# TensorE reads x with a step, from rows that land in zeroed buffers, in a kernel of attention and a state-space convolution mixed by a gate

## The chip, the cores and the metric

The kernel runs on one core of a Trainium2 chip, in one launch. The metric is the device time of that core in microseconds. A profiled execution gives, beside its time, the span from the first to the last instruction and a record of every instruction. The engines are named TensorE (PE in the profile, with its weight loads as PEld), VectorE (DVE), ScalarE (ACT), GpSimd (POOL) and SyncE (SP).

## The reference

The sequence has 2048 rows of 512 channels. Branch a is attention with 32 heads of 16, without a mask. Branch b is a diagonal state-space convolution of the same x along the sequence: for each channel a kernel K of length 2048 is made from 128 complex modes, and y is the causal convolution of K and x. A sigmoid gate of x mixes both.

```python
def _A_ref(x, wqkv, wo):                        # H = 32, Dh = 16
    q, k, v = split(x @ wqkv)
    p = softmax(einsum("bhqd,bhkd->bhqk", q, k) * Dh ** -0.5)
    return (p @ v).reshape(B, S, D) @ wo

def _B_ref(u, A_re, A_im, B_re, B_im, C_re, C_im, log_dt, Dskip):
    dt = exp(log_dt)[:, None]
    P = exp((dt * A)[:, :, None] * arange(L))
    K = einsum("dn,dnl,dn->dl", C, P, dt * Bc).real
    y = causal_convolution(K, u)                # by FFT in the reference
    return y + u * Dskip

x = A_x
g = sigmoid((x * gate_w).sum(-1, keepdims=True))
return g * _A_ref(x, ...) + (1 - g) * _B_ref(x, ...)
```

## The kernel before

**Attention.** The scores of one head for 512 queries and 128 keys are a slot; there are 2048 slots. A quad is four slots (four heads, one tile of keys). ScalarE takes the slots in groups of three: one instruction exponentiates 1536 columns from one of two PSUM buffers, SC0 and SC1, into the ring ET (`ex`, L705). TensorE makes the scores of the next group meanwhile (`qk`, "SC<-Qm,KT"), then PV (`pv`, "OA<-ET,VE"). Some quads are given to VectorE: then a group has two slots for ScalarE (1024 columns) and one that VectorE exponentiates by a polynomial in five instructions (`exp_in` L715, `exp_out` L725 to L732, result ED). Every 16 quads a block of queries is done: VectorE transposes OA (`norm_a`, L749), and TensorE's next PV waits for that. Qm (L681) is the masked Q of the next block.

**Convolution, in chunks of 64 rows.** Channels are taken in 16 blocks of 32, four blocks to a quarter. `params` and `base` make powers of the modes on VectorE; `base` ends a quarter with a cast (L944). `table` multiplies them out into PT (L968 copies, then six triples of two products tt and one PT, L763) and stores PT to DRAM (gm_ptd). `kstage` makes the taps of a block on TensorE ("MB<-PT,wrb" and "MB<-PT,nwi", eight matmuls) and stores a padded form (gm_kpd). `qload` reads PT back transposed (Qt). `sstage` makes, per block and in four banks, what each chunk adds to the state: 128 matmuls of 64 columns with x as the moving operand ("MB<-XZ,Qt"), and VectorE moves each bank to SG (L1051). `scan` runs over the 31 chunks in order on VectorE, five instructions a step (L1074 to L1087, the last a cast to SG). `ystage` makes y in 32 units: eight matmuls of 32 columns with x and the taps ("MB<-X,Tt"), then 32 with the states ("MB<-SG,Py", the moving operand read with a step of 288 elements).

**x for the convolution.** At the start x is copied to DRAM reordered (gm_xrd). For each quarter `ublocks` transfers two halves of 64 partitions into XS by SyncE's queue. VectorE gathers them so that the 32 chunks of a channel lie together (XP, L1178, two instructions), and writes two masked copies, one for each half of the partitions, into XZ (L1189, with the masks hm), so that one product of 64 columns keeps the two channels apart. `ulocal` transfers the same rows again into XR, and VectorE gathers them into X2 (L1178) for `ystage`.

**The order of the work.** The program for every engine is written out ahead by a planner (`Sched`). Each stage is a generator that yields the engine and an estimated cost of its next piece. After every exponential group the planner issues pieces whose inputs it thinks ready (`fill`), and pads TensorE with products of zeros ("OA<-wm") up to an amount of columns for each group. `dve_slot` gives VectorE a quad only when the taps of all blocks are done ("K15") and no quarter stands between its last state product and the end of its scan. The engines run their lists in order, with semaphores. SBUF is placed after planning (`place`): buffers whose lives don't meet share bytes, and the first use of one then waits for the last use of the other.

In `record`, what the change touches: the masks hm (L640, L641), the list of buffers (L991), the moving operands in `sstage` (L1047) and `ystage` (L1143), `rows` (L1170), `ublocks` (L1181) and `ulocal` (L1193).

```python
lambda k=k: XZ[qr](64 * (16 * bl + k), [[1, 64]]),
...
lambda kk=kk: X2[qr](32 * (16 * bl + kk), [[1, 32]]),
```

Of the kernel before, what the change touches and what calls it, by code (L numbers as in the profile page):

```python
# [6 lines left out]
FP32 = mybir.dt.float32  # L7
# [6 lines left out]
S = 2048  # L14
# [366 lines left out]
def declare(nc, es):  # L381
    B = {}

    def sb(name, free, dt=BF16):
        B[name] = Buf(name, "sb", free, dt)


    sb("KT", 4 * S)
    for k in range(16):
        sb(f"Q{k}", 512)  # L390
        sb(f"OnT{k}", 512)
    sb("Qm", 2 * 512)
    sb("VE", 64 * VW)
    sb("ET", NS * 512)
    sb("OT", 512, FP32)
    sb("ON", 512)
    sb("Rz", 2 * 16, FP32)
    sb("Wo", 4 * D)
    sb("xT", 4 * S)
    for n in ("Wk", "Wq", "Wv"):  # L400
        sb(n, 4 * D)
    sb("msk", 2, FP32)
    sb("sgn", 2, FP32)
    sb("hm", 2, FP32)
    sb("piota", 4, FP32)
    sb("hpi", 1, FP32)
    for k in range(EW):
        sb(f"eL{k}", 512, FP32)
    sb("em", 512, FP32)
    sb("eu", 512, FP32)  # L410
    sb("ED", 4 * 512)

    sb("gwT", 4)
    sb("wm", D)
    sb("x0n", 4 * D)
    sb("idf", P, FP32)
    sb("idb", P)
    sb("gp", NCH, FP32)
    sb("ge", NCH, FP32)
    sb("g", NCH, FP32)  # L420
    sb("g1", NCH, FP32)
    sb("Dpb", 16)
    sb("Dp", 16, FP32)
    sb("Yl", 16 * D)
    sb("fo", 4 * D)
    sb("fp", 4 * D, FP32)

    for n in ("AreT", "AimT", "BreT", "BimT", "CreT", "CimT", "ldt", "dt"):
        sb(n, D)
    for n in ("an", "bn", "ba", "ea", "e2", "sb_", "cb", "u1", "u2", "u3", "u4", "zr", "zi"):  # L430
        sb(n, D, FP32)
    sb("wrb", D)
    sb("nwi", D)
    sb("VV", 2 * D, FP32)
    sb("VL", 2 * D, FP32)
    for n in ("L1", "L2", "L4", "L8", "L16", "L32", "L48"):
        sb(n, 2 * D, FP32)
    sb("MU", 3 * D, FP32)
    sb("pt1", 2 * D, FP32)
    sb("pt2", 2 * D, FP32)  # L440
    for n in ("D16", "D32", "D48"):
        sb(n, 2 * 2 * D)

    sb("FP", 2 * 128 * 8, FP32)
    sb("ft1", 2 * 64 * 8, FP32)
    sb("ft2", 2 * 64 * 8, FP32)
    for k in range(4):
        sb(f"B16{k}", 2 * 128 * 16)

    sb("PT", 2 * 2 * CB * T)  # L450
    sb("tt1", 2 * CB * 16)
    sb("tt2", 2 * CB * 16)
    sb("Qt", 2 * 32 * 128)
    sb("Kst", 2 * 8 * P)

    for k in range(NSG):
        sb(f"SG{k}", NCH * 2 * SGH)
    sb("G", 2 * 128, FP32)
    for n in ("s2", "s3"):
        sb(n, 2 * 128, FP32)  # L460

    for k in range(4):
        sb(f"X2{k}", 32 * 64)
        sb(f"XZ{k}", 2 * 32 * 64)
        sb(f"XS{k}", 32 * 64)
        sb(f"XP{k}", 32 * 64)
        sb(f"XR{k}", 32 * 64)

    sb("Py", 3 * 2 * 16 * T)
    sb("Tt", 3 * 8 * 128)  # L470
    for i in range(2):
        B[f"SC{i}"] = Buf(f"SC{i}", "ps", 1536, FP32)
    B["OA"] = Buf("OA", "ps", 512, FP32)
    B["MB"] = Buf("MB", "ps", 512, FP32)
    for n, free in (("ptd", NBLK * P * 2 * CB * T), ("kpd", NBLK * P * 8 * P), ("xrd", S * D)):
        B[n] = Buf(n, "dr", free, BF16)
        B[n].t = nc.dram_tensor("gm_" + n, [free // P, P], BF16)
    for n in ("SC0", "SC1", "OA", "MB"):
        B[n].t = es.enter_context(nc.psum_tensor(n, [P, B[n].free], FP32))
    for n in ("x", "w", "wo", "are", "aim", "bre", "bim", "cre", "cim", "ldt_d", "dsk_d", "gw_d", "out"):  # L480
        B["d_" + n] = Buf("d_" + n, "dr", 1, BF16)
    return B
# [79 lines left out]
def record(nc, p, B, ins):  # L562
# [73 lines left out]
    for k in range(1, 8):  # L636
        op("DVE", lambda v, k=k: v.scalar_tensor_tensor(
            pio(1 + k % 2, [[1, 1]]), pio(0, [[1, 1]]), 16.0 * k, pio(1 + (k - 1) % 2, [[1, 1]]), ALU.is_ge, ALU.add),
           [(pio, 0), (pio, 1 + (k - 1) % 2)], [(pio, 1 + k % 2)], c=.17)
    op("DVE", lambda v: v.tensor_scalar(B["hm"](0, [[1, 1]]), pio(0, [[1, 1]]), 64.0, None, ALU.is_lt), [(pio, 0)], [(B["hm"], 1)], c=.17)  # L640
    op("DVE", lambda v: v.tensor_scalar(B["hm"](1, [[1, 1]]), pio(0, [[1, 1]]), 64.0, None, ALU.is_ge), [(pio, 0), (B["hm"], 1)], [(B["hm"], 0)], c=.17)  # L641
    op("DVE", lambda v: v.memset(B["sgn"](0, [[1, 1]]), 1.0), [], [(B["sgn"], 1)])
    op("DVE", lambda v: v.memset(B["sgn"](1, [[1, 1]]), -1.0), [(B["sgn"], 1)], [(B["sgn"], 0)])
    op("DVE", lambda v: v.memset(msk(0, [[1, 2]]), 0.0), [], [(msk, 0)])
# [343 lines left out]
                sch.add(qload(blk), 3)  # L988
                sch.add(kstage(blk), .5)

    X2, XZ = [B[f"X2{k}"] for k in range(4)], [B[f"XZ{k}"] for k in range(4)]  # L991

    def qload(blk):
        yield ("AFTER", f"S{blk - 2}" if blk >= 2 else "base1")
# [34 lines left out]
    def sstage(blk):  # L1029
# [8 lines left out]
        for bank in range(4):  # L1038
            yield ("LOCK", "MB")
            for k4 in range(4):  # L1040
# [3 lines left out]
                for ri in range(2):  # L1044
                    mm(lambda k4=k4, ri=ri: MB(256 * ri + 64 * k4, [[1, 64]]),
                       lambda k=k, ri=ri: Qt(q0 + 2048 * ri + 128 * k, [[1, 128]]),
                       lambda k=k: XZ[qr](64 * (16 * bl + k), [[1, 64]]),  # L1047
                       [(Qt, (blk % 2, 2 * ri + k // 8), blk), (XZ[qr], 0), (XZ[qr], 1)], [(MB, 0, ('S', blk, bank))],
                       c=.1 if k4 % 2 == ri == 0 else .07, a=64)
            yield ("DVE", .66, -1)  # L1050
            op("DVE", lambda v, bank=bank: v.tensor_tensor(sg(2 * SGH + CB * bl + 8 * bank, [[2 * SGH, 31], [SGH, 2], [1, 8]]),  # L1051
# [74 lines left out]
    def ystage():  # L1126
        yield ("AFTER", "gp")

        def unit(u):
# [8 lines left out]
            for k in range(8):  # L1138
                if k % 4 == 0:
                    yield ("PE", .28, 2, True)  # L1140
                kk = 8 * hf + k
                mm(lambda k=k: MB(32 * k, [[1, 32]]), lambda k=k: Tt(r * 1024 + 128 * k, [[1, 128]]),
                   lambda kk=kk: X2[qr](32 * (16 * bl + kk), [[1, 32]]),  # L1143
                   [(X2[qr], 0), (X2[qr], 1)] + [(Tt, (r, par, k // 4), u) for par in range(2)] + [(Tt, "z")], ky, k == 0, False, c=.1 if k % 4 == 0 else .06, a=32)
            for k in range(8):
                if k % 2 == 0:
                    yield ("PE", .48, 2, True)
# [17 lines left out]
        for u in range(2 * NBLK):  # L1165
            yield from unit(u)

    hm = B["hm"]

    def rows(b, o, qr):  # L1170
        for par in range(2):
            yield ("SP", 1.9)
            dma("SP", lambda e, par=par: e.dma_start(b(0, [[64, 32], [1, 64]], 64 * par, 64),
                                                     B["xrd"].dram(64 * qr + 256 * par, [[32 * D, 64], [D, 32], [1, 64]])),
                [(B["xrd"], 0)], [(b, par)], c=1.9, lat=5)
        for k in range(2):
            yield ("DVE", 1.15)
            op("DVE", lambda v, k=k: v.tensor_copy(o(1024 * k, [[32, 32], [1, 32]]), b(32 * k, [[1, 32], [64, 32]])),  # L1178
               [(b, 0), (b, 1)], [(o, k)], c=1.15)

    def ublocks(qr):  # L1181
        XS, XP = B[f"XS{qr}"], B[f"XP{qr}"]
        yield ("AFTER", f"yu{8 * qr - 12}" if qr >= 2 else f"S{4 * qr - 2}" if qr else "base3")
        yield from rows(XS, XP, qr)
        if qr:
            yield ("AFTER", f"S{4 * qr - 1}")
        for h in range(2):
            yield ("DVE", .75)
            op("DVE", lambda v, h=h: v.tensor_scalar(XZ[qr](32 * h, [[64, 64], [1, 32]]), XP(0, [[32, 64], [1, 32]]), hm(h, [[1, 1]]), None, ALU.mult),  # L1189
               [(XP, 0), (XP, 1), (hm, 0)], [(XZ[qr], h)], c=.75)  # L1190
        sch.mark(f"ub{qr}")

    def ulocal(qr):  # L1193
        yield ("AFTER", f"S{4 * qr + 3}")
        yield ("AFTER", "K15")
        yield from rows(B[f"XR{qr}"], X2[qr], qr)
        sch.mark(f"ul{qr}")

    def ublks():
# [296 lines left out]
    g = 0  # L1496
# [73 lines left out]
```

## Time and profile before

| | us |
|---|---|
| median of 3 runs | 922.45 (921.2 to 922.65) |
| the profiled execution, time | 923.37 |
| its span | 921.6 |
| ScalarE busy | 900.0 |
| VectorE busy | 807.1 |
| TensorE busy (matmuls) | 788.7 |
| GpSimd busy | 14.6 |
| granted TensorE clock, mean | 0.99 |

A line of a group of instructions reads: line of the code, engine, operation, output<-inputs, shapes, count, then busy time and mean duration of one in ns, then the idle time of the engine just ahead of them and what ended it. A wait reads: who, "<-" what it waited for, us in total, how often, the longest. A timeline gives start and duration ahead of the same names. Instructions of one engine overlap a little, so a mean duration is longer than the distance from one to the next; a piece "x8" is eight in a row.

### The profile page before, as it was taken

The page shows a single profiled execution, that of the slowest core. Times are in us where ns is not written, and L with a number is a line of the kernel's source. Part 1 is how long each engine was busy: PE and PEld are TensorE (multiplying, and loading weights), DVE is VectorE, ACT ScalarE, POOL GpSimd, SP SyncE. Part 2 cuts the span into 40 slices and gives each one's busy share as a digit, 9 for nine tenths or more (in the row PEclk, how much of TensorE's full clock was granted, in tenths as well). Part 3 has the DMA queues.
Part 4 walks back from the last instruction along what each step waited for, and adds up shares of the span by engine and source line. Part 5 has one row for each costly group of instructions (what it writes and reads, how often), then busy time and mean ns, then how long its engine had stood idle before and what let it go on. Part 6 is the DMA issues. An engine that isn't in the chain of part 4 may idle for free.

```text
span 921.6 us, 18065 instructions
## 1 busy us (share of the span) xinstructions
PE 788.7 (86%) x7521; PEld 266.4 (29%) x7521; DVE 807.1 (88%) x1653; ACT 900.0 (98%) x693; POOL 14.6 (2%) x16
## 2 busy tenths in 40 slices
PE   7899988878888787878999878998889899999884
PEld 3233232222222222222333322333233333333321
DVE  5799999997778999999998888899899987888885
ACT  6999999999999999999999999999999999999995
POOL 4000000000000000010000000000000000000000
PEclk9999999999899999999999999999999999999998
DMA  9300000016859557562242267336312232201101
GB/s 194 98 1 1 1 1 1 1 24 163 201 146 211 157 142 114 149 195 52 58 110 58 61 102 104 92 76 115 59 30 72 82 100 59 58 7 31 34 1 24
DMA packets 171473, 73.40 MB, mean 80 GB/s; under 512 B 150272, under 2 KB 159104, under 8 KB 169344
## 3 DMA queue, kind: packets, MB, share of 16 engines
q1 hardware_dynamic: 169088, 71.07, 33.1%
q10 hardware_dynamic: 2304, 1.18, 0.7%
q8 instruction: 59, 0.97, 0.4%
q14 instruction: 22, 0.18, 0.1%
HBM read 30.02 MB, written 25.17 MB: 60 GB/s over the span
## 4 chain that ended last, share of the span: by engine, by line
ACT 87%; DVE 7%; PE 3%; DMA 2%; issue 0%; ACTq 0%; SPq 0%; DVEq 0%
ACT ET L705 87%; DVE ft L763 2%; DVE tt L763 2%; PE OA L577 1%; PE SC L577 1%; DMA gm_ptd<-PT 1%; DMA Wq<-in_A_wqkv_dram 1%; DVE PT L763 1%; PE MB L577 1%; DVE B L763 1%; DVE FP L763 0%; DVE fo L1250 0%; DVE B L944 0%; DVE XP L1178 0%; DVE FP L921 0%
## 5 line engine op out<-in xcount | busy, mean ns | idle before, releaser
L705 ACT ACTIVATE ET<-SC 128x1536 bf16<-128x1536 f32 (+1 forms) x683 | 892.8, 1836 | 5.5 <-PE SC L577 5.5
L577 PE MATMUL SC<-Qm,KT 32*128 32x512 bf16 x2048 | 267.7, 386 | 110.2 <-ACT ET L705 91.6
L577 PE MATMUL OA<-wm 128*128 128x512 bf16 (+8 forms) x785 | 242.0, 367 | 2.6 <-DVE OT L749 1.4
L577 PE MATMUL OA<-ET,VE 128*32 128x512 bf16 x1988 | 198.3, 391 | 1.7 <-DVE OT L749 1.0
L577 PEld LDWEIGHTS SC<-Qm,KT 32*128 32x128 bf16 x2048 | 66.3, 91 | 332.3 <-ACT ET L705 319.4
L577 PEld LDWEIGHTS OA<-ET,VE 128*32 128x32 bf16 x1988 | 50.7, 93 | 120.0 <-issue 114.4
L577 PEld LDWEIGHTS OA<-wm 128*128 128x128 bf16 x785 | 55.2, 97 | 83.5 <-issue 69.2
L715 DVE TENSOR_SCALAR eL<-SC 128x512 int32<-128x512 f32 x60 | 41.3, 688 | 26.2 <-PE SC L577 25.7
L763 DVE TENSOR_TENSOR tt<-B,D 128x1024 bf16<-128x1024 bf16 x96 | 62.4, 685 | 0.5
L1084 DVE TENSOR_TENSOR G<-s,s 128x256 f32<-128x256 f32 x120 | 50.7, 423 | 3.3
L577 PE MATMUL MB<-SG,Py 128*64 128x32 bf16 x1024 | 50.7, 230 | 0.0
L1080 DVE TENSOR_TENSOR s<-s,SG 128x256 f32<-128x256 f32 x120 | 50.2, 418 | 0.0
L1077 DVE TENSOR_TENSOR s<-G,MU 128x256 f32<-128x256 f32 x120 | 50.2, 418 | 0.0
L1074 DVE TENSOR_TENSOR s<-G,MU 128x256 f32<-128x256 f32 x120 | 50.1, 418 | 0.0
L1051 DVE TENSOR_TENSOR SG<-MB,sgn 128x496 bf16<-128x496 f32 x64 | 42.9, 670 | 6.9 <-PE MB L577 6.1
L732 DVE SCALAR_TENSOR_TENSOR ED<-eu,eL 128x512 bf16<-128x512 f32 x60 | 41.3, 688 | 1.3
L730 DVE SCALAR_TENSOR_TENSOR eu<-eu,em 128x512 f32<-128x512 f32 x60 | 41.2, 686 | 1.4
L728 DVE SCALAR_TENSOR_TENSOR eu<-em 128x512 f32<-128x512 f32 x60 | 41.1, 685 | 0.9
L577 PEld LDWEIGHTS MB<-SG,Py 128*64 128x64 bf16 x1024 | 30.5, 116 | 28.0 <-issue 27.8
L1087 DVE CAST SG<-G 128x256 bf16<-128x256 f32 x120 | 35.4, 295 | 3.2
L749 DVE STREAM_TRANSPOSE OT<-OA 128x512 f32<-128x512 f32 x32 | 22.9, 715 | 13.4 <-PE OA L577 13.0
L763 DVE TENSOR_TENSOR ft<-FP,L 128x1024 f32<-128x1024 f32 (+1 forms) x32 | 34.1, 1085 | 0.4
(136 smaller groups left out, 563.9 us busy)
## 6 DMA issues: line engine op xcount, KB each, us to landing
gm_ptd<-PT SPq DMA_DIRECT2D x16, 1024.0 KB, 5.9
Py<-gm_ptd SPq DMA_DIRECT2D x32, 512.0 KB, 4.1
gm_kpd<-Kst SPq DMA_DIRECT2D x16, 256.0 KB, 4.3
Tt<-gm_kpd SPq DMA_DIRECT2D x128, 32.0 KB, 3.3
gm_xrd<-in_A_x_dram SPq DMA_DIRECT2D x1, 2048.0 KB, 12.1
XS<-gm_xrd SPq DMA_DIRECT2D x8, 256.0 KB, 4.2
XR<-gm_xrd SPq DMA_DIRECT2D x8, 256.0 KB, 4.4
out_dram<-fo SPq DMA_DIRECT2D x28, 64.0 KB, 2.1
```

Of the source, the lines that this page charges most:

```text
L577: op("PE", lambda t: t.matmul(out(), lhsT(), rhs(), start=start, stop=stop, skip_group_check=True, **kw), R, W, c=c, lat=.15, a=a)
L705: op("ACT", lambda a: a.activation(ET(512 * e, [[1, 512 * n]]), sc(0, [[1, 512 * n]]), AF.Exp, scale=DH ** -0.5), [(sc, i, g) for i in ran ...
L715: op("DVE", lambda v: v.tensor_scalar(eL.int(0, one), sc(512 * i, one), DH ** -0.5 / math.log(2) * 2 ** 23, EXP0, ALU.mult, ALU.add), [(sc ...
L728: op("DVE", lambda v: v.scalar_tensor_tensor(eu(0, one), em(0, one), r2, em(0, one), ALU.add, ALU.mult), key("em"), key("eu"), c=.69)
L730: op("DVE", lambda v: v.scalar_tensor_tensor(eu(0, one), eu(0, one), r1, em(0, one), ALU.add, ALU.mult), key("em", "eu"), key("eu"), c=.69)
L732: op("DVE", lambda v: v.scalar_tensor_tensor(ED(512 * (d % 4), one), eu(0, one), r0, eL(0, one), ALU.add, ALU.mult), key("eu") + [(eL, 0, ...
L763: op(eng, lambda v: v.tensor_tensor(o(), a(), b_(), f), R, W, c=c)
L1051: op("DVE", lambda v, bank=bank: v.tensor_tensor(sg(2 * SGH + CB * bl + 8 * bank, [[2 * SGH, 31], [SGH, 2], [1, 8]]), MB(0, [[1, 31], [256 ...
L1074: op(e, lambda v: v.tensor_tensor(s2(0, [[128, 2], [1, 128]]), G(0, [[128, 2], [1, 128]]), MU(d0, [[0, 2], [1, 128]]), ALU.mult), key("G", ...
L1077: op(e, lambda v: v.tensor_tensor(s3(0, [[128, 2], [1, 128]]), G(128, [[-128, 2], [1, 128]]), MU(D + d0, [[D, 2], [1, 128]]), ALU.mult), k ...
L1080: op(e, lambda v, so=so: v.tensor_tensor(s2(0, [[128, 2], [1, 128]]), s2(0, [[128, 2], [1, 128]]), sg(so, [[SGH, 2], [1, 128]]), ALU.add), ...
L1084: op(e, lambda v: v.tensor_tensor(G(0, [[1, 256]]), s2(0, [[1, 256]]), s3(0, [[1, 256]]), ALU.add), [(s2, 0), (s3, 0)], [(G, 0)], c=.38)
```

## The change

VectorE's part in bringing x is dropped, and with it hm, XS, XP and X2. For the state products a memset on GpSimd clears XZ (4096 columns) once for each quarter, and the two transfers write their 64 partitions straight into XZ: the first half of the partitions into the first 2048 columns, the second half into the second 2048, so that the zeros do what the masks did. TensorE reads XZ as two runs of 32 columns with a step of 64 elements between columns. For the taps products TensorE reads XR with the same step, 32 columns. `ublocks` also drops its wait for the state products of the quarter before, and the transfers into XZ wait for the memset. Nothing else is edited; the planner makes a new order from it.

```diff
-                       lambda k=k: XZ[qr](64 * (16 * bl + k), [[1, 64]]),
-                       [(Qt, (blk % 2, 2 * ri + k // 8), blk), (XZ[qr], 0), (XZ[qr], 1)], [(MB, 0, ('S', blk, bank))],
+                       lambda k=k: XZ[qr](16 * bl + k, [[XH, 2], [64, 32]]),
+                       [(Qt, (blk % 2, 2 * ri + k // 8), blk), (XZ[qr], 0), (XZ[qr], 1), (XZ[qr], "z")], [(MB, 0, ('S', blk, bank))],
...
-                   lambda kk=kk: X2[qr](32 * (16 * bl + kk), [[1, 32]]),
+                   lambda kk=kk: XR[qr](16 * bl + kk, [[64, 32]]),
...
-    def rows(b, o, qr):
+    def rows(b, qr, half):
         for par in range(2):
             yield ("SP", 1.9)
-            dma("SP", lambda e, par=par: e.dma_start(b(0, [[64, 32], [1, 64]], 64 * par, 64),
+            dma("SP", lambda e, par=par: e.dma_start(b(half * par, [[64, 32], [1, 64]], 64 * par, 64),
                                                      B["xrd"].dram(64 * qr + 256 * par, [[32 * D, 64], [D, 32], [1, 64]])),
-                [(B["xrd"], 0)], [(b, par)], c=1.9, lat=5)
-        for k in range(2):
-            yield ("DVE", 1.15)
-            op("DVE", lambda v, k=k: v.tensor_copy(o(1024 * k, [[32, 32], [1, 32]]), b(32 * k, [[1, 32], [64, 32]])),
-               [(b, 0), (b, 1)], [(o, k)], c=1.15)
+                [(B["xrd"], 0)] + ([(b, "z")] if half else []), [(b, par)], c=1.9, lat=5)
 
     def ublocks(qr):
-        XS, XP = B[f"XS{qr}"], B[f"XP{qr}"]
         yield ("AFTER", f"yu{8 * qr - 12}" if qr >= 2 else f"S{4 * qr - 2}" if qr else "base3")
-        yield from rows(XS, XP, qr)
-        if qr:
-            yield ("AFTER", f"S{4 * qr - 1}")
-        for h in range(2):
-            yield ("DVE", .75)
-            op("DVE", lambda v, h=h: v.tensor_scalar(XZ[qr](32 * h, [[64, 64], [1, 32]]), XP(0, [[32, 64], [1, 32]]), hm(h, [[1, 1]]), None, ALU.mult),
-               [(XP, 0), (XP, 1), (hm, 0)], [(XZ[qr], h)], c=.75)
+        yield ("POOL", 4.)
+        op("POOL", lambda g: g.memset(XZ[qr](0, [[1, 2 * XH]]), 0.0), [], [(XZ[qr], "z")], c=4.)
+        yield from rows(XZ[qr], qr, XH)
         sch.mark(f"ub{qr}")
 
     def ulocal(qr):
...
-        yield from rows(B[f"XR{qr}"], X2[qr], qr)
+        yield from rows(XR[qr], qr, 0)
```

## The prediction

> **What bounds the kernel now.** I read the page's busy shares first, then its chain of work that ended last, then the waits, then the groups of instructions kept apart by shape, and last the timelines around the places that the change touches.
>
> ```profile
> PE 788.7 (86%) x7521; PEld 266.4 (29%) x7521; DVE 807.1 (88%) x1653; ACT 900.0 (98%) x693; POOL 14.6 (2%) x16
> ACT 87%; DVE 7%; PE 3%; DMA 2%; issue 0%; ACTq 0%; SPq 0%; DVEq 0%
> PEld SC L577 <- ACT ET L705: 319.4, 636, 1.2
> ACT ET L705 <- PE SC L577: 5.5, 6, 3.3
> ```
>
> ScalarE is the bound: 98% busy, 87% of the chain. Its exponentials (L705) are idle 5.5 us in all, 3.3 of it at the start. TensorE waits for ScalarE 319.4 us before QK products, 0.47 us for each of 683 groups. VectorE matters only through two things: how many score slots it takes off ScalarE, and whether it is late with something TensorE stands waiting for, because TensorE works in order and the next QK is behind.
>
> **What a slot is worth.** From the chain in order of time (start, us, what):
>
> ```profile
> 18.50 143.70 ACT ET L705 x107
> 536.15 300.44 ACT ET L705 x235
> ```
>
> The first piece holds only three-slot groups: 143.70/107 = 1.343 us. The second holds 36 two-slot groups: (300.44 - 199 x 1.343)/36 = 0.92 us. A slot given to VectorE saves 0.42 us.
>
> **What the change removes.** 8 gathers XS to XP, 8 gathers XR to X2, 8 masks:
>
> ```profile
> L1178 DVE COPY XP<-XS 128x1024 bf16<-128x1024 bf16 x8 | 8.2, 1049 | 0.0
> L1178 DVE COPY X<-XR 128x1024 bf16<-128x1024 bf16 x8 | 8.0, 1040 | 0.0
> L1189 DVE TENSOR_SCALAR XZ<-XP,hm 128x2048 bf16<-128x2048 bf16 x8 | 5.8, 754 | 0.0
> ```
>
> That is 22 us of VectorE, off the bound by itself. The planner spends it: in the order of the changed kernel's instructions VectorE has 64 exponential slots in place of 60, ScalarE 618 three-slot and 65 two-slot groups in place of 622 and 61. 4 x 0.42 = **-1.7 us**, and this gain is on the bound.
>
> **A stall that should go.** In ScalarE's timeline from 225 us:
>
> ```profile
> 237.12 1.45 ACT L705 ACTIVATE ET<-SC 128x1536 bf16<-128x1536 f32 x1 [0.94 <-PE SC L577]
> 238.75 1.45 ACT L705 ACTIVATE ET<-SC 128x1536 bf16<-128x1536 f32 x1 [0.18 <-PE SC L577]
> 240.69 20.25 ACT L705 ACTIVATE ET<-SC 128x1536 bf16<-128x1536 f32 x15 [0.49 <-PE SC L577]
> ```
>
> 0.94 + 0.18 + 0.49 = 1.6 us. TensorE stood 1.65 us at 234.3 us before the second bank of block 0's state products, waiting for VectorE's eviction (L1051), which was behind table work that had waited 2.0 us for a table transfer (PT to gm_ptd) to land. After it TensorE ran at a reduced clock (0.87 granted in 220 to 240 us; a QK took 0.61 us, 0.39 before). Changed, the table work has no gathers in it and its transfer goes out earlier against that eviction: I take **-1.6 us**; the bound on the other side is 0, the stall staying.
>
> **What it adds on GpSimd.** Four memsets of 4096 columns. The nearest row is Tt's, 3072 in 2.66 us: 0.865 ns each, so 3.54 us. GpSimd is idle, but look at VectorE beside Tt's memset (from the timeline of all engines, start and duration first):
>
> ```profile
> 395.18 2.66 POOL L1120 MEMSET Tt<- 128x3072 bf16 x1 [104.77 <-DVE tt L763]
> ...
> 395.38 0.69 DVE L763 TENSOR_TENSOR PT<-tt,tt 128x1024 bf16<-128x1024 bf16 x1
> ...
> 396.77 0.42 DVE L1084 TENSOR_TENSOR G<-s,s 128x256 f32<-128x256 f32 x1
> ...
> 397.23 0.76 DVE L1087 CAST SG<-G 128x256 bf16<-128x256 f32 x1
> ```
>
> The products kept their usual times (0.69, 0.42). The cast, 0.29 us in the mean of 120, took 0.76 and ended at 397.99, just after the memset's end at 397.84. One event, but it reads as a cast that stood until the memset was done. So each new memset can hold VectorE by up to 3.54 us where a cast or a like operation meets it.
>
> Second memset (XZ1). In GpSimd's order it follows the clearing of SG0, which waits for the last VectorE product that reads L8 (SG0 lies over L8). That product ends at 197.46 us before; with 0.2 us to wake and 0.34 for SG0 the memset runs from 198.0 to 201.5. It meets the last cast of the base stage, same operation and types as the one above:
>
> ```profile
> 198.83 1.22 DVE L944 CAST B<-FP 128x2048 bf16<-128x2048 f32 x1
> ...
> 216.41 0.40 PE L577 MATMUL MB<-PT,wrb 128*32 128x512 bf16 x4
> ```
>
> It would end at 202.6, 2.6 us late. Behind it stand the copies and six triples of table products: start to start 1.13 + 0.67 + 6 x 2.06 = 14.2 us, so without the memset PT is complete at 213.0 (215.7 before), with it at 215.6. Block 0's taps (216.41 above) wait for PT, and the planner has moved them three groups forward for the VectorE time it thinks saved: 216.41 - 3 x 1.343 + 0.33 for the PV now ahead = 212.7. TensorE stands there 2.9 us. Then 0.45 for the taps, 0.44 for fillers, 0.43 for QK: scores at 216.9, due at 214.75. That is 2.2 us, and about 0.6 more for the reduced clock, as after the stall above (0.18 + 0.49). The first memset (XZ0, released by the last gate product at 184.06, so 184.4 to 187.9) may hold a small tensor_scalar at 187.30 by 0.6 us in the same VectorE chain; I add half. **+3.1 us**, bounds 0 and 4.
>
> Third (XZ2), released by the last taps product of block 15, with the scan running. A scan step has a cast every 1.79 us (624.75 to 626.54), so 3.54 us of memset always meets one and costs VectorE 1.75 to 3.54. In the order a Qm and the transpose of OA come two casts later, and TensorE's next PV waits for that transpose. The cover is 0.47 us of TensorE's slack and QK's lead. **+1.4**, bounds 0 and 2.6. Fourth (XZ3), released by block 11's last state product, with two offloaded slots unfinished whose PV TensorE meets soon: **+0.8**, bounds 0 and 2.5. Tt's memset moves into the table stage and meets at most the scan's first cast; I take 0, its cover being that 0.47 per group.
>
> The row shows only a cast. [...]
>
> **What it adds on TensorE.** x is now read with a step of 64 elements. The nearest rows (mean ns after the bar):
>
> ```profile
> L577 PE MATMUL MB<-SG,Py 128*64 128x32 bf16 x1024 | 50.7, 230 | 0.0
> L577 PE MATMUL MB<-XZ,Qt 128*128 128x64 bf16 x512 | 29.7, 195 | 1.9 <-DVE SG L1051 1.7
> L577 PE MATMUL MB<-X,Tt 128*128 128x32 bf16 x256 | 12.8, 178 | 0.2 <-DVE SG L1051 0.2
> ```
>
> Py's product reads SG with a step (288 elements): 52 ns more than X's for the same 32 columns, 1.6 ns a column. Sixteen of them take 0.62 us, eight 0.40: 55 ns a pair of halves, 1.7 ns a column again. At that price an XZ product (64 columns, 30 ns of stream now) takes 109, an X product (26 now) 55: 512 x 79 + 256 x 29 ns = 48 us of TensorE. Lower bound 0 (the step is nothing, Py's time is its halves), upper twice it. The 319.4 us cover it on the whole. From 525 to 565 us, the densest state stretch, TensorE waits 15.1 us for ScalarE and holds 13 groups of eight: 13 x 0.63 = 8.2. It fits, with some bursts; a QK may also be about 0.8 us late before ScalarE feels it. **+1.0**, bounds 0 and 5. State and taps products now wait for the transfer of x itself instead of a gather or mask after it; these landed in 4.2 and 4.4 us and are issued tens of us ahead (XS at 184.4, first used at 232.5): 0. SP issues the same 16 transfers; the eight into XZ now wait for a memset, at the front of SP's queue, but the memsets end well ahead of the issue of table loads behind them: 0.
>
> **Sum.** -1.7 - 1.6 + 3.1 + 1.4 + 0.8 + 1.0 = +3.0. The profiled execution took 923.37 us (span 921.6, 1.8 around it), so 926.4 by it; it lies 0.9 above the median of the runs, 922.45, so the median becomes **925.5 us**. About 0.2% (1.85 us) is what a measurement of this kernel can tell from no change.
>
> **Rivals.** (1) The memsets don't hold VectorE, or TensorE's slack hides it: for it, one event is all there is; against it, the cast's end just behind the memset's. Only gains and half of the bursts remain: 922.45 - 3.3 + 0.5 = 919.7, faster. 0.25. (2) Only the second memset hurts, since the third and fourth fall where nothing of TensorE waits: 922.45 - 3.3 + 3.1 + 0.5 = 922.8. 0.17. (3) TensorE becomes the bound in the state stretches: it decides once a group of eight costs over 15.1/13 = 1.16 us more, 1.8 times my price; at twice (1.26 and little slack left for bursts) some 3 us in each of two dense stretches: about 931. 0.10. (4) The change doesn't do what it says for the time: slots gained and stalls cancel, 922.5. 0.03. The forecast has 0.45; its own range is 924 to 928.
>
> **Range and chances.** 919 to 930 takes in (1), (2) and part of (3). Faster: 0.25 from (1). Same: (2), (4) and 0.02 of the forecast's lower end, 0.22. Slower: the rest, 0.53.
>
> **What would show it.** Four memsets of 3.5 us on GpSimd. The L944 cast near 199 us with over 3 us; if it has 1.2, the forecast's main term is gone. TensorE waiting 2 to 3 us for PT before block 0's taps; ScalarE's wait for QK from 5.5 to some 10 us; a scan cast of 2 us or more near 387 us and an L725 near 537. MB<-XZ at about 275 ns, the taps product at about 205 to 230. 65 two-slot groups. Wrong would be: ScalarE idle no more than before, or idle beside XZ products rather than beside waits for VectorE.

## The result and the profile after

The changed kernel took 960.18 us (median of 4 runs, 951.0 to 965.99) against 922.55 before (921.2 to 924.96): **slower, by a ratio of 1.0329 (95% interval 1.0305 to 1.0353)**. Two of these four runs were disturbed, as was one run each of experiment 6, of kept_gather and of gpsimd_gather; the ratios and the times of those experiments leave them out, and of gpsimd_gather, whose profiled execution it was, only what stands ahead of 361 us is read. The two others here took 951.0 and 955.08. The profiled execution took 951.0, with a span of 949.2, 27.6 longer than before. The forecast was 925.5, its range ended at 930, and rival (3), the dearest, stood at 931.

The page of the changed kernel, busy shares, granted clock in 40 slices, and the chain that ended last by engine:

```profile
PE 852.8 (90%) x7502; PEld 305.9 (32%) x7502; DVE 807.4 (85%) x1647; ACT 903.9 (95%) x693; POOL 28.9 (3%) x20
...
PEclk9999999998986979999999976999999999999997
...
ACT 68%; PE 17%; DVE 12%; DMA 2%; issue 1%; ACTq 0%; SPq 0%; DVEq 0%
```

ScalarE's share fell from 98% to 95% and its part of the chain from 87% to 68%; TensorE's part rose from 3% to 17%. TensorE is busy 64.1 us longer. The row of the granted clock is new: slices with 6, 7 and 8 between 210 and 360 us and between 545 and 595. The waits (in total, how often, the longest):

```profile
PEld SC L573 <- ACT ET L699: 248.6, 525, 1.1
...
ACT ET L699 <- PE SC L573: 27.3, 43, 3.0
```

The bound engine waits for TensorE 27.3 us (5.5 before), and TensorE still waits 248.6 us for ScalarE. Both hold at once: an engine with a quarter of its span to spare in the mean is late in 43 places. Of ScalarE's idle time after 20 us, 24.3 us in 42 gaps (2.2 in 5 before), the timeline has 4.7 in five gaps between 192 and 223 us, 1.1 at 412, 9.8 between 256 and 351, 2.0 between 543 and 553, 5.0 between 567 and 587, and 1.7 scattered.

The three casts and tensor_scalars that the prediction expected to be held are there. From the chain in order of time (start, us):

```profile
199.27 3.54 DVE B L938
...
405.76 2.35 DVE SG L1082
...
560.61 2.63 DVE em L719
```

GpSimd cleared XZ from 198.22 to 201.73, from 404.46 to 407.97 and from 559.45 to 562.96 (3.51 us each); the cast of the base stage has 1.2 us elsewhere, the scan's 0.29 and the masking step 0.42, and each of the three ended only behind the memset's end (at 202.8, 408.1 and 563.2). The instruction of em at 560.53 is a tensor_scalar; its whole time was 2.71 us, of which the chain counts 2.63, so it was held as the two casts were. Not everything of their kinds was: before has three tensor_scalars of one column (hm at 2.71 and 2.89 us, msk at 4.00) beside the memsets of VE (1.47 to 9.79), each of 0.15 us, and there too three casts of xT out of SC and MB (5.67 to 7.73) of 0.68 to 0.69 each, as long as Kst's casts of the same shape take elsewhere (0.69).

What nobody expected stands in TensorE's timeline, here from 272.8 us:

```profile
272.83 1.05 PE L573 MATMUL MB<-XZ,Qt 128*128 128x64 bf16 x8
273.81 0.39 PE L573 MATMUL SC<-Qm,KT 32*128 32x512 bf16 x3
...
276.70 0.61 PE L573 MATMUL SC<-Qm,KT 32*128 32x512 bf16 x3
277.24 1.01 PE L573 MATMUL OA<-wm 128*128 128x512 bf16 x2
278.18 0.61 PE L573 MATMUL SC<-Qm,KT 32*128 32x512 bf16 x3
278.72 0.62 PE L573 MATMUL OA<-ET,VE 128*32 128x512 bf16 x4
279.27 1.05 PE L573 MATMUL MB<-XZ,Qt 128*128 128x64 bf16 x8
```

Eight state products hold TensorE 0.98 us (272.83 to 273.81; 0.24 before), just as priced. Then QK goes from 0.39 us to 0.61 (from its start to the next product's, 0.32 to 0.54), and PV and the zeros slow down as well: the granted clock of 280 to 300 us is 0.50. No idle time stands ahead of it from 272.8 us on. Counting as half clock each stretch in which a QK triple takes over 0.5 us, before has one of 5.0 us (after the 1.65 us stall at 234) and after has eight, 83 us together, of 27.2, 20.7 and 13.7 us and shorter. The stepped group itself takes 1.05 at both clocks (at 272.83 and at 279.27), so the clock doesn't set its time.

### The profile page after: what moved, and what is told of

Its sections match the earlier page's. It is cut to its first block, busy times and chain, and to the rows that moved or that the text cites. A ratio compares the mean times of both kernels' runs of the same rounds, so it can differ in the third digit from the quotient of the medians.

```text
span 949.2 us, 18016 instructions
## 1 busy us (share of the span) xinstructions
PE 852.8 (90%) x7502; PEld 305.9 (32%) x7502; DVE 807.4 (85%) x1647; ACT 903.9 (95%) x693; POOL 28.9 (3%) x20
## 3 DMA queue, kind: packets, MB, share of 16 engines
q10 hardware_dynamic: 2304, 1.18, 0.6%
## 4 chain that ended last, share of the span: by engine, by line
ACT 68%; PE 17%; DVE 12%; DMA 2%; issue 1%; ACTq 0%; SPq 0%; DVEq 0%
ACT ET L699 68%; PE OA L573 7%; PE MB L573 5%; PE SC L573 5%; DVE tt L757 2%; DVE ft L757 2%; DVE PT L757 1%; DVE SG L1046 1%; DMA Wq<-in_A_wqkv_dram 1%; DMA gm_ptd<-PT 1%; DVE B L757 1%; DVE B L938 0%; DVE fo L1234 0%; DVE FP L757 0%; DVE Kst L1013 0%
## 5 line engine op out<-in xcount | busy, mean ns | idle before, releaser
L699 ACT ACTIVATE ET<-SC 128x1536 bf16<-128x1536 f32 (+1 forms) x683 | 896.7, 1651 | 28.2 <-PE SC L573 27.3
L573 PE MATMUL SC<-Qm,KT 32*128 32x512 bf16 x2048 | 276.8, 399 | 65.0 <-ACT ET L699 48.7
L573 PE MATMUL OA<-wm 128*128 128x512 bf16 (+5 forms) x766 | 247.8, 383 | 2.5 <-DVE OT L743 1.3
L573 PE MATMUL OA<-ET,VE 128*32 128x512 bf16 x1984 | 204.7, 404 | 4.7 <-DVE OT L743 4.1
L573 PEld LDWEIGHTS SC<-Qm,KT 32*128 32x128 bf16 x2048 | 66.6, 91 | 293.0 <-ACT ET L699 248.6
L573 PE MATMUL MB<-XZ,Qt 128*128 128x64 bf16 x512 | 70.4, 286 | 2.0 <-DVE SG L1046 0.7
L709 DVE TENSOR_SCALAR eL<-SC 128x512 int32<-128x512 f32 x64 | 44.1, 689 | 25.7 <-PE SC L573 25.3
L1046 DVE TENSOR_TENSOR SG<-MB,sgn 128x496 bf16<-128x496 f32 x64 | 43.0, 672 | 20.7 <-PE MB L573 19.8
L573 PEld LDWEIGHTS MB<-XZ,Qt 128*128 128x128 bf16 x512 | 47.1, 111 | 24.5 <-issue 18.4
L726 DVE SCALAR_TENSOR_TENSOR ED<-eu,eL 128x512 bf16<-128x512 f32 x64 | 43.9, 687 | 1.4
L722 DVE SCALAR_TENSOR_TENSOR eu<-em 128x512 f32<-128x512 f32 x64 | 43.9, 686 | 1.2
L724 DVE SCALAR_TENSOR_TENSOR eu<-eu,em 128x512 f32<-128x512 f32 x64 | 43.9, 686 | 1.2
```

The source lines that it names most:

```text
L573: op("PE", lambda t: t.matmul(out(), lhsT(), rhs(), start=start, stop=stop, skip_group_check=True, **kw), R, W, c=c, lat=.15, a=a)
L699: op("ACT", lambda a: a.activation(ET(512 * e, [[1, 512 * n]]), sc(0, [[1, 512 * n]]), AF.Exp, scale=DH ** -0.5), [(sc, i, g) for i in ran ...
L709: op("DVE", lambda v: v.tensor_scalar(eL.int(0, one), sc(512 * i, one), DH ** -0.5 / math.log(2) * 2 ** 23, EXP0, ALU.mult, ALU.add), [(sc ...
L722: op("DVE", lambda v: v.scalar_tensor_tensor(eu(0, one), em(0, one), r2, em(0, one), ALU.add, ALU.mult), key("em"), key("eu"), c=.69)
L724: op("DVE", lambda v: v.scalar_tensor_tensor(eu(0, one), eu(0, one), r1, em(0, one), ALU.add, ALU.mult), key("em", "eu"), key("eu"), c=.69)
L726: op("DVE", lambda v: v.scalar_tensor_tensor(ED(512 * (d % 4), one), eu(0, one), r0, eL(0, one), ALU.add, ALU.mult), key("eu") + [(eL, 0, ...
```

## The experiments

Line numbers are those of the kernel of each run; in the diffs, "..." marks lines left out. (There are 32 state products to a block, 128 to a quarter; the text ahead gives 128 to a block.) "Half clock" is counted as above, over one profiled execution.

**1. Adjacent columns, the memsets kept.**

```diff
-                       lambda k=k: XZ[qr](16 * bl + k, [[XH, 2], [64, 32]]),
+                       lambda k=k: XZ[qr](64 * (16 * bl + k), [[1, 64]]),
...
-                   lambda kk=kk: XR[qr](16 * bl + kk, [[64, 32]]),
+                   lambda kk=kk: XR[qr](32 * (16 * bl + kk), [[1, 32]]),
```

> The changed kernel, its order of instructions untouched, but TensorE reads XZ and XR without a step, and so other columns of x than it should (the convolution is made from the wrong elements). Memsets as changed. Theory STEP (the stepped reads and the reduced clock that comes with them cost most of the 28 us): about 926 us, since only the held casts are left (4 us at block 0's taps, some 1 us each at the other memsets, against 1.7 for the slots and 1.6 for the stall that went); mean granted clock 0.98 or more; MB<-XZ back at about 195 ns. Theory MEMSET (VectorE held by the memsets makes TensorE idle, that lowers the clock, and the rest follows): 943 to 951 us.

931.78 us (930.94 to 935.54), ratio 1.0103 (1.0077 to 1.013). That lies between the two theories. The steps are worth some 20 us, the rest 9 against before. Half clock is 40.8 us in five stretches, and four of them begin behind an idle TensorE. It waits 1.27 us at 188.5 and 2.24 at 394.9 for the transpose of OA, each time behind an instruction that a memset had held (a tensor_scalar at 186, the scan's cast at 391; in the changed kernel, which has the same order, they took 0.72 and 2.35 us), and 1.38 at 551.5 for Yl, behind the em held at 544 (2.71 us in the changed kernel). The 1.43 us at 269.6 are not the memsets' doing: an eviction (L1046) is late there, behind table work that had waited 1.52 us for the transfer of PT. The fifth, at 457, has no wait over 0.8 us ahead of it.

**2. The memsets in pieces, the steps kept.**

```diff
-        op("POOL", lambda g: g.memset(XZ[qr](0, [[1, 2 * XH]]), 0.0), [], [(XZ[qr], "z")], c=4.)
+        for i in range(16):
+            op("POOL", lambda g, i=i: g.memset(XZ[qr](256 * i, [[1, 256]]), 0.0), [], [(XZ[qr], "z")], c=.25)
```

> The changed kernel with each memset of XZ cut into 16 of 256 columns, so that a cast of VectorE need not stand for 3.5 us; all else and the other engines' order untouched, stepped reads kept. STEP: 940 to 946 us (951 less the 4.0 at block 0's taps, 1.1 at the scan's cast and part of what follows the held masking step near 560 us), clock still under 0.97 with stretches at half clock around 280 to 350 us. MEMSET: 920 to 924 us, clock 0.99. The longest L939 or so base cast falls from 3.6 us to under 1.6; if it doesn't, pieces don't free VectorE.

942.85 us (931.47 to 944.0), ratio 1.0182 (1.0122 to 1.0242). The runs differ as their clocks do: three took 941.75 to 944.0 us at a mean granted clock of 0.950 to 0.958, one 931.47 at 0.980. VectorE is free: the longest L938 cast is 1.22, the longest scan cast 0.42. The loss stays for the most part, and so does half clock, 72.8 us in the profiled execution (941.75).

**3. Both:** the edits of 1 and 2 together.

> Both of the above: no step in the reads (other columns of x than it should), memsets in 16 pieces. Both theories: 919 to 920.5 us (922.5 less 1.7 for four slots and up to 1.6 for the old stall), clock 0.99. If it stays above 922, the gain that the prediction booked for the slots or the stall isn't there.

920.63 us (919.6 to 923.66, 10 runs), ratio 0.9972 (0.9961 to 0.9983): faster than before, by 0.3%. No half clock; from the waits:

```profile
ACT ET L699 <- PE SC L573: 4.4, 6, 2.6
```

So the gains of the prediction were there, 2.4 us of its 3.3, and the loss is whole in the steps and the memsets: 22.2 us for the steps (942.85 - 920.63; 10.8 by the run of 931.47), 11.2 for the memsets (931.78 - 920.63); together, in the changed kernel, 30 to 34 (951.0 and 955.08 against 920.63).

**4. TensorE as long at work, at full rate:** as 3, each state product issued four times.

```diff
-        op("PE", lambda t: t.matmul(out(), lhsT(), rhs(), start=start, stop=stop, skip_group_check=True, **kw), R, W,
+        op("PE", lambda t: [t.matmul(out(), lhsT(), rhs(), start=start, stop=stop, skip_group_check=True, **kw) for _ in range(rep)][-1], R, W,
...
-                       c=.1 if k4 % 2 == ri == 0 else .07, a=64)
+                       c=.1 if k4 % 2 == ri == 0 else .07, a=64, rep=4)
```

> As the one before (no step, memsets in pieces), but every XZ product is issued four times over, each rewriting the same columns: TensorE is taken up about as long as by the stepped reads (4 x 27 to 30 ns against 109), while it streams four times the columns. STEP with the clock following the columns streamed: clock 0.98 or more and 920 to 926 us, far below the kernel with stepped reads and memsets in pieces. Theory TIME (only TensorE's lost time counts, and the clock falls because TensorE gets late and disturbed): about the same as that kernel, 938 to 946 us, with half-clock stretches.

926.94 us (925.77 to 928.02), ratio 1.0039 (1.0026 to 1.0052), no half clock. TensorE is held at least as long as by the stepped products, which are busy 70.4 us:

```profile
L573 PE MATMUL MB<-XZ,Qt 128*128 128x64 bf16 x2048 | 74.4, 193 | 5.0 <-DVE SG L1046 4.0
```

TensorE's time alone costs 6.3 us (1.5 of ScalarE's idle time in it, at 306, lies behind an eviction that came late). That is six times the term of the prediction, and a quarter of what the steps cost.

**5 and 6. One step at a time,** with the memsets in pieces: only XR, then only XZ, read with the step (to the edit of 2, the first pair of lines of 1's diff alone is added, then the second alone).

> The changed kernel with the memsets in 16 pieces; only the taps products read x with the step, the state products read 64 adjacent columns (other columns of x, so the state is left out as a result). unit_step_pieces, with neither step, took 920.6 us, memset_pieces, with both, 942.9: 22 us for the two steps. If the cost goes by TensorE's added time, it is shared as the added time is: the page gives 96 ns more for a state product (193 to about 288, 512 of them, 49 us) and about 50 ns more for a taps product (256 of them, 13 us), so the taps have 13/62 of 22 = 4.6 us: 925. If it goes by stretches in which the granted clock falls, and these come where stepped products are packed eight to a group, it depends on where they stand: the taps products stand eight in a row once per unit with 32 others behind them, so I expect no half-clock stretch and at most 1 to 2 us: 921 to 922.5.

> The changed kernel with the memsets in 16 pieces; only the state products read x with the step, the taps products read 32 adjacent columns (other columns of x, so the local part of y is left out as a result). By TensorE's added time: 49/62 of 22 us = 17.4, so 938. By the clock: nearly all of it, 940 to 942, with half-clock stretches of 50 us or more in all as in memset_pieces (72.8), inside the stretches of state products.

Taps alone: 922.68 (919.68 to 923.75, 10 runs), 2.0 more than 3, half clock 5.4 us. State products alone: 940.02 (934.39 to 948.32, three runs), about as dear as both, half clock 97 us in the profiled execution, the longest of the three. By TensorE's added time the taps should have had 4.6.

**7. More zeros beside the stepped products** (as 2, everything computed): the planner is told that they stream nothing.

```diff
-                       c=.1 if k4 % 2 == ri == 0 else .07, a=64)
+                       c=.1 if k4 % 2 == ri == 0 else .07, a=0)
```

> memset_pieces (nothing left out: the whole computation, both steps) with one edit: the planner is told that a state product streams 0 columns instead of 64, so it pads the groups that hold state products with up to 512 more columns of zeros products (36 thousand columns more in all, 353 to 389 thousand). If the 16 us that occupancy doesn't explain come from the granted clock falling where few columns are streamed, the zeros hold it up: half-clock stretches fall from 73 us to under 25 and the time from 942.9 to 926 to 934. If the stepped reads cost by TensorE's time alone, the zeros add 36 thousand x 0.42 ns = 15 us of TensorE in its tightest groups: the same 943 or more, up to 950.

937.88 us (933.47 to 941.48), ratio 1.0178 (1.0157 to 1.02). The median fell by 5 us only, above the band of the first theory and below that of the second. But the four runs don't share a clock: the profiled one took 933.47 us at 0.989, with 3.8 us of half clock where experiment 2 has 72.8, the others 937.14 to 941.48 at 0.973 to 0.981. Zeros buy the clock, not in every run, and pay for it in TensorE's time.

**8. The same with adjacent columns:** as 4, with the edit of 7.

> pieces_more_zeros with adjacent columns (other columns of x, so y is left out as a result) and each state product issued four times, so that TensorE has as much to do in the same order, but every column streams at its full rate. pieces_more_zeros took 937.9 (933.5 to 941.5) with only 3.8 us of half clock in its profile; repeat_unit_step, without the added zeros, 926.9. If what is left in pieces_more_zeros is TensorE's time alone, this takes 931 to 937 too. If the stepped reads cost something beside their time that the zeros don't mend, it takes 927 to 930.

935.23 us (933.63 to 936.25), half clock 3.7 us, granted clock 0.990 to 0.993. The run of 7 at 0.989 took 933.47, so with the clock held up a stepped product costs what its time costs and no more that shows. The zeros cost 8.3 (935.23 - 926.94).

**9. Few columns in the same time:** as 3, with three products of 8 columns ahead of each state product.

```diff
-                       c=.1 if k4 % 2 == ri == 0 else .07, a=64)
+                       c=.1 if k4 % 2 == ri == 0 else .07, a=64,
+                       few=3 * ((lambda k4=k4, ri=ri: MB(256 * ri + 64 * k4, [[1, 8]]), lambda k=k: XZ[qr](64 * (16 * bl + k), [[1, 8]])),))
```

(`mm` issues the products in `few` ahead of its own.)

> unit_step_pieces (adjacent columns, other ones of x, so y is left out as a result) with three products of 8 columns ahead of each state product of 64, so that TensorE has about as long to do (the taps products of 32 columns take 26 ns each in a row; 30 + 3 x 26 = 108 ns, as a stepped product) but streams 88 columns in that time and not 256 as in repeat_unit_step. That took 926.9 us with no half-clock stretch, the stepped reads 942.9 with 73 us of them. If the granted clock goes by the columns streamed, few_columns falls too: half-clock stretches of over 30 us in all and 935 to 945. If it is the stepped read itself that lowers it, 925 to 929 and none. If a product of 8 columns takes much less than 26 ns, TensorE's time is not matched, and 921 to 926 says nothing.

931.54 us (929.73 to 931.79), ratio 1.0094 (1.0081 to 1.0107). TensorE's time is matched (a group of eight holds it 0.94 us):

```profile
228.71 1.01 PE L573 MATMUL MB<-XZ,Qt 128*128 128x8 bf16 x32
229.65 0.39 PE L573 MATMUL SC<-Qm,KT 32*128 32x512 bf16 x3
```

Half clock came, without any stepped read of x: 26.9 us from 270.3 on. All four runs granted 0.978 to 0.982, against 0.987 to 0.994 in 4. Both expectations missed: the fall is there, but a third of the stepped kernel's. It comes behind a wait, so idle time would be a rival cause; but experiment 4 has nearly the same wait at the same place and keeps its clock. First 9, then 4:

```profile
269.44 0.71 PE L573 MATMUL MB<-XZ,Qt 128*128 128x8 bf16 x16 [1.36 <-DVE SG L1047]
...
270.30 0.61 PE L573 MATMUL SC<-Qm,KT 32*128 32x512 bf16 x3
```

```profile
269.66 0.64 PE L573 MATMUL MB<-XZ,Qt 128*128 128x64 bf16 x16 [1.18 <-DVE SG L1046]
...
270.35 0.39 PE L573 MATMUL SC<-Qm,KT 32*128 32x512 bf16 x3
```

**10. One long memset:** as 3, XZ1 cleared in one piece.

```diff
-        for i in range(16):
-            op("POOL", lambda g, i=i: g.memset(XZ[qr](256 * i, [[1, 256]]), 0.0), [], [(XZ[qr], "z")], c=.25)
+        for i in range(1 if qr == 1 else 16):
+            n = 4096 if qr == 1 else 256
+            op("POOL", lambda g, i=i, n=n: g.memset(XZ[qr](n * i, [[1, n]]), 0.0), [], [(XZ[qr], "z")], c=4. * n / 4096)
```

> unit_step_pieces (adjacent columns, so y is left out as a result) with one of its four memsets in one piece again, that of XZ1, which meets the cast of the base stage. The prediction gave this memset 2.2 us of lateness and 0.6 for the clock, 2.8 in all: 920.6 + 2.8 = 923.4. If the clock's fall after the idle of TensorE costs more than 0.6, 925 or more; in unit_step all four together cost 11 us where the prediction gave 5.3.

923.87 us (922.3 to 924.58, 10 runs), ratio 1.0013 (0.9999 to 1.0028): 3.2 more than 3, where the prediction had 2.8. From TensorE's timeline:

```profile
214.87 0.62 PE L573 MATMUL MB<-PT,wrb 128*32 128x512 bf16 x4 [2.62 <-DVE PT L757]
```

TensorE stands 2.62 us for PT and comes back at half clock for 4.2 us, as the prediction had it (2.9, and 0.6 of ScalarE's time for the clock; ScalarE's gaps here are 3.31, 0.63 and 0.40).

**11. The price by the step:** the kernel before, the step of the state products by block.

```diff
-                       lambda k=k: XZ[qr](64 * (16 * bl + k), [[1, 64]]),
+                       lambda k=k: XZ[qr](16 * bl + k, [[(1, 2, 4, 8, 16, 32, 64)[blk % 7], 64]]),
```

> The kernel before with the state products of block b reading x at a step of 1, 2, 4, 8, 16, 32, 64 elements, by b modulo 7 (other columns of x, so y is left out as a result). One look, for the price of a product by step. At 1.7 ns a column from some step on, a product has 193 to 195 ns at step 1 and about 285 at 64. [...]

935.38 us in one run. Pieces of eight, steps 2, 4 and 8:

```profile
248.08 0.42 PE L577 MATMUL MB<-XZ,Qt 128*128 128x64 bf16 x8
...
272.59 0.64 PE L577 MATMUL MB<-XZ,Qt 128*128 128x64 bf16 x8
...
283.34 1.09 PE L577 MATMUL MB<-XZ,Qt 128*128 128x64 bf16 x8
```

Eight take 0.41 at step 1, then 0.42, 0.64 and 1.09, and 1.10, 1.04, 1.05 at 16, 32 and 64. With fours (0.29, 0.30, 0.40, 0.62, and 0.60 at 64) one more product costs 30 ns at steps 1 and 2, 60 at 4, 118 at 8, 112 at 64. Step 2 is free and all from 8 elements on cost alike, 1.8 ns a column.

**12 to 15. Kernels that compute everything.** Three search for the gain of 3. *taps_step_only* is before with XR read with the step and its gathers dropped. *kept_gather* stores XP once and loads it again as X2, so the second gather goes and all columns stay adjacent; *kept_gather_early* also drops the masks' wait for the quarter before. *gpsimd_gather* moves gathers and masks to GpSimd in pieces. All have 65 two-slot groups. The three parts of the diff are the read of taps_step_only, the load of kept_gather and the masks of gpsimd_gather.

```diff
-                   lambda kk=kk: X2[qr](32 * (16 * bl + kk), [[1, 32]]),
+                   lambda kk=kk: XR[qr](16 * bl + kk, [[64, 32]]),
...
-        yield from rows(B[f"XR{qr}"], X2[qr], qr)
+        dma("SP", lambda e: e.dma_start(X2[qr](0, [[1, 2048]]), B["xpd"].dram(qr * P * 2048, [[2048, P], [1, 2048]])),
+            [(B["xpd"], qr)], [(X2[qr], 0), (X2[qr], 1)], c=.5, lat=4)
...
+                op("POOL", lambda g, h=h, k=k: g.tensor_scalar(XZ[qr](512 * k + 32 * h, [[64, 8], [1, 32]]), XS(8 * k, [[1, 8], [64, 32]]), hm(h, [[1, 1]]), None, ALU.mult),
+                   [(XS, 0), (XS, 1), (hm, 0)], [(XZ[qr], h)], c=.5)
```

> The kernel before with the change done for the taps products alone: they read XR with the step of 64 elements and the eight gathers XR to X2 go; XZ is gathered and masked by VectorE as before, no memset of XZ is added, nothing is left out. The order has 65 two-slot groups, as many as the whole change has: 4 slots more than before, -1.7 us. If the whole change was bad through its state products and memsets, this part alone is a gain: 922.5 to 923 before, so 920 to 922. If stepped taps products cost TensorE by its time (about 13 us in all, 4.6 us of the end by share), it is slower than before: 924 to 926.

> Nothing left out. The kernel before, with the gather done once: XP, which VectorE makes for the state products, is stored to DRAM and loaded again as X2 for the taps products, in place of loading the rows and gathering them a second time. Eight gathers go (8 us of VectorE), one store and one load for each quarter stand for two row transfers, TensorE reads adjacent columns, no memset is added. The order has 65 two-slot groups. By the slots 922.5 - 1.7 = 920.8; taps_step_only had the same slots and took 926.4, of which the stepped taps products have about 2 and waits of ScalarE near 835 us (1.95 and 1.15) most of the rest. If these came with the steps, this takes 920 to 922; if they come with the planner's denser order of VectorE's exponentials, 923 to 925.

> kept_gather, and the masked copies no longer wait for the last state product of the quarter before (as in the whole change). Nothing left out. It shifts the order only; 65 two-slot groups or near. As kept_gather within 2 us: 919 to 924. Faster than before, if the stall near 237 us or those near 835 us move off VectorE's late places; no theory says which.

> Nothing left out. The kernel before, with VectorE's gathers and masks of x moved to GpSimd in pieces of 256 columns (16 masked copies for each XZ, 8 copies for each X2), so that TensorE goes on reading adjacent columns and VectorE is rid of the 22 us. The order has the 65 two-slot groups of the whole change. If the loss of the change lies in the stepped reads and the long memsets, and not in what VectorE gave up, this takes what unit_step_pieces took, 920.6 us, plus at most 2 for pieces that hold VectorE's casts: 920 to 923 against 922.6 before. If GpSimd's pieces are slow (no row shows such a copy; a memset of 256 columns took 0.22 us) and VectorE stands by them, it is 924 or more, and the casts at L944 and L1087 show maxima far above 1.2 and 0.4 us.

taps_step_only 926.38 (926.17 to 927.03), ratio 1.0041 (1.0029 to 1.0054); kept_gather 925.2 (922.76 to 928.91, 10 runs), ratio 1.0033 (1.0017 to 1.0048); kept_gather_early 921.95 (920.31 to 928.02, 11 runs), ratio 0.9998 (0.9984 to 1.0012); gpsimd_gather 967.65 (964.9 to 970.14, 4 runs), ratio 1.0493 (1.0464 to 1.0522). The first two came out on the dear sides of their expectations. They share their stalls: in both ScalarE's timeline has the old stall near 236 us (0.98 and more) and new ones of 0.3, 0.8 and 1.95 us near 533, 671 and 833. The last comes as TensorE waits 1.55 us (1.56 in kept_gather) for the last ED of an offloaded quad at the end of a query block, with QK behind. As kept_gather has no stepped read of x, these stalls are the order's doing, not the steps': the four slots are worth their 1.7 us only if the order has VectorE in time. kept_gather_early is the best kernel that computes everything, and equals before; none beats it.

Of gpsimd_gather, the stretch from 186 to 218 us:

```profile
L1189 POOL TENSOR_SCALAR XZ<-XS,hm 128x256 bf16<-128x256 bf16 x16 | 26.6, 1666 | 178.7 <-DMA XS<-gm_xrd 177.4
```

A masked copy of 256 columns takes GpSimd 1.67 us (a memset of 256 takes 0.34 in the mean, not the 0.22 of the expectation), 27 us for a quarter, and VectorE's pairs of tt products beside it take 1.6 to 1.7 where they had 1.29. ScalarE then stands 6.66 us at 220 us. The dear side of its expectation came.

## Why the prediction was wrong

**Right, in mechanism and size.** The price of a stepped product: 109 ns forecast, 112 to 118 for one more in a row (experiment 11), 286 ns for one with its latency (275 forecast); 232 for a taps product (205 to 230). The slots and the stall: -3.3 forecast, -2.4 measured in experiment 3; the stall at 237 us is gone. The second memset: +2.8 forecast, +3.2 measured alone. The scan's cast: 1.08 us of ScalarE's idle at 412, +1.4 forecast. XZ0's memset: the tensor_scalar at 187 held by 0.55 us (0.6 forecast), 0.7 us of idle at 192 (0.3 forecast). That +0.3 and the +0.8 of XZ3 took it that a tensor_scalar is held as the scan's cast was; no run of before shows that. The changed kernel does: 0.72 us for 0.17 at 187.11, 2.71 for 0.42 at 560.53.

**Wrong: the step "+1.0, covered" on TensorE.** The prediction laid 48 us of work against 319.4 us of waits and found a stretch of 15.1 us against 8.2. Two things failed in it, and a third beside it, in the memsets' terms.

First, the cover was counted over a stretch, where it has to lie in the same group as the work or just behind it, because TensorE works in the order of its list: the QK behind the eight products of 272.83 started at 273.81. Eight stepped products hold TensorE 0.74 us longer, and a group's slack was 0.47 in the mean. Rival (3) put the turning point at 1.16 us more a group; at 0.80 more (experiment 4: 1.04 against 0.24) TensorE's time already cost 6.3 us, and 5.0 of the 5.9 us of ScalarE's gaps of experiment 4 lie in the stretches with state products (251 to 306, 511 to 528 and 627 to 646 us). The term was too small by a factor of six.

Second, and larger: the sum held the granted clock fixed, but for 0.6 us after one stall. The products of a group make their columns slower, so fewer columns are streamed in a microsecond, and the clock fell to half for 83 us. There three QK take 0.61 us for 0.39, four PV 0.62 for 0.40 and two products of zeros 1.01 for 0.60, nothing is left of the slack, and ScalarE waits. With TensorE's time for a group about the same, the time follows the half clock:

| state products, memsets in pieces | columns streamed for each | group of eight, us | half clock, us | time, us |
|---|---|---|---|---|
| experiment 4 | 256 | 1.04 | 0 | 926.94 |
| experiment 9 | 88 | 0.94 | 26.9 | 931.54 |
| experiment 2 | 64 | 0.98 | 72.8 | 942.85 |

Experiments 7 and 8 close it from the other side: where zeros hold the clock up, stepped and adjacent products cost the same (933.47 against 933.63 to 936.25). I count 6.3 us for TensorE's time and some 16 for what the clock takes; the second goes with the clock of the run and is 4.5 in the run of experiment 2 that kept 0.980. At that clock nothing is left for the stepped read itself: 931.47 us there, 929.73 to 931.79 in experiment 9 at 0.978 to 0.982.

Third, the memsets' price left out what a stall does to the clock. One alone cost 3.2; all four, with adjacent columns, 11.2 where the sum had 5.3. Experiment 1 has half-clock stretches at 191, 398, 457 and 556 us (35 of its 41 us) that experiment 10 lacks; all but the one at 457 begin behind waits that lead back to a held instruction. XZ3 was put at 0.8; behind the held em of 560.61 half clock began at 566.6 and ScalarE lost 5.0 us up to 587.

**The sum again, by measured terms:** -2.4 for slots and stall, +22.2 for the steps, and some 10 for the memsets (951.0 and 955.08 against 942.85) give about +30; 922.55 became 951 and 955. The memsets' term is what is left here, so the sum has to come out; measured by itself, with adjacent columns, it was 11.2. The text named the right sign of being wrong, "idle beside XZ products rather than beside waits for VectorE", and gave the case 0.10.

The clock can be followed further. Its records in the traces (gpsimd_gather left aside) say full or half and nothing between, and every stretch is a whole number of 3.41 us on one grid that runs through the execution (in the changed kernel 27.3 us from 276.2 on, 13.7 from 337.6, 20.5 from 566.3).

So what TensorE did in each step of that grid, a window of 3.41 us, can be counted. I take the windows between 24 and 860 us, spread each product evenly over its record, and weigh its columns by the size of its weights as the trace writes them: QK with 32*128 and PV with 128*32 count a quarter, a state product or one of zeros with 128*128 counts whole. In before, after and experiments 5, 6, 7, 9 and 12 to 14, the 25 windows ahead of a fall hold 542 to 903 such columns a microsecond (903 in the changed kernel, from 272.8 us on); of the 2,106 others at full clock only four hold less than 903, the least 889 (before, from 306.6 us on; the median of all is 1,171). The border is the same for stepped and adjacent reads: falls up to 857 and none from 897 on in experiment 6, 757 and 898 in experiment 9. A stepped read then counts by its few columns, and nothing here asks for more. Without the weights the windows don't part: falls come behind up to 2,873 columns a microsecond, and 1,864 passes; in experiment 4 the window from 303.3 us on has 1,360 plain and 1,022 weighted, and passes. What stays open is what sets the border. In experiments 1 to 4, 8, 10 and 11, which ran on other chips than 5 to 7, 9 and 12 to 14, falls come behind 419 to 863, but windows down to 740 pass.

A fall needs no long idle time ahead of it: one came behind 0.80 us (experiment 2, at 267.0), and the one at 276.70 above behind none.

## What to carry to other kernels

Ask of a slower operand not only whether its time fits in TensorE's waits, but whether it fits in the same group, and how many columns a microsecond are left, each weighed by the size of its weights: this kernel, which pads with zeros, has about 1,170 in the median, and its clock fell where what streams few columns took it to 903 or less. Read the row of the granted clock for each stretch in every prediction that lengthens TensorE's work. The long memset on GpSimd, which kept the base cast at 3.62 us, let it go at 1.22 when it was cut into sixteen pieces; masked copies on GpSimd are another matter (VectorE's pairs of tt products took 1.6 to 1.7 us beside them, 1.29 without).

## What the runs showed of the hardware

- In experiment 11 a moving operand in bf16 costs nothing more at a step of 2 elements (30 ns for 64 columns), twice at 4 (60), nearly four times (112 to 118, 1.8 ns a column) from 8 elements on, and then the same up to 64; in the changed kernel eight products at 64 take 1.05 us at full and at half clock. Of the steps tried only 2 is free.
- Sixteen memsets of 256 columns in place of one of 4096 take GpSimd 5.88 to 6.21 us in place of 3.51 (experiment 10), and VectorE's casts no longer wait (in experiment 2 1.22 and 0.42 us at most, against 3.62 and 2.35 in the changed kernel).
- The falls of the granted clock went by what TensorE streams, not by idle time alone: at the same place in the order one came behind 0.80 us of idle among stepped products (experiment 2) and not behind 1.18 us among products at full rate (experiment 4).
